# Retention and a Mish feed-forward on one core: two phases through HBM, or one interleaved loop kept on chip

## The chip, the core and the metric

The kernel runs on one core of a Trainium2 chip. A core has a matrix engine (TensorE, PE in the rows; its weight loads are shown as PEld), a vector engine (VectorE, DVE), an activation engine (ScalarE, ACT), a general engine (GpSimd, POOL) and a queue engine that only issues transfers (SyncE, SP). They run independently and wait for each other through semaphores. Matmuls write to PSUM, a small memory of eight banks; everything else lies in SBUF, and transfers (DMA) move data between SBUF and HBM. The metric is the device time of the whole program in microseconds (us), lower is better.

## What is computed

Eight batches of eight heads, 576 positions, head size 64. First a retention (attention without softmax, with a decay per head), then a feed-forward layer over all 4608 tokens with the Mish activation, `h * tanh(log(1 + exp(h)))`:

```python
scores = (q @ k.transpose(0, 1, 3, 2)) / sqrt(64)          # per batch b, head h: 576 x 576
gamma  = 1.0 - 2.0 ** (-5.0 - arange(8))                   # one decay per head
Dmat   = where(i >= j, gamma ** (i - j), 0.0)              # i: query position, j: key position
attn   = (scores * Dmat) @ v                               # 576 x 64 per head
x      = attn.transpose(0, 2, 1, 3).reshape(4608, 512)     # tokens x (head, dim)
h      = x @ w_in                                          # 512 -> 2048
out    = (h * tanh(softplus(h))) @ w_out                   # 2048 -> 512, float32
```

Inputs and output are float32; the kernel multiplies in bfloat16.

## The kernel before

One function with two phases, one after the other.

*Retention phase* (lines 50 to 126). A loop over the 8 heads builds `Lcat`, the decays of all distances of that head (L57 to L61). Inside, a loop over the 8 batches handles one (batch, head) pair, 64 in all. The 576 positions are cut into blocks of 128, 128, 128, 128 and 64. For each block `q` and `k` are loaded by POOL with a cast to bfloat16 (L74, L75), transposed on PE into one PSUM tile `tpqk` (L77, L78; a single buffer), and copied out by DVE (`qTall` L79, `kT` L81); `v` is loaded by SP (L84) and scaled by ACT (`vb` L86). Then PE computes the scores of each key block against all later queries (`Tp`, L99), DVE multiplies them by the decays (`Tm`, L104), PE multiplies with `vb` into five output tiles (`opsum`, L115), DVE copies them (L123), and SP stores them as 128 x 64 pieces into `x_bridge`, a float32 tensor in HBM (L124).

*Feed-forward phase* (lines 128 to 197). The weights are loaded by POOL with a cast, 64 pieces of `w_in` (L139) and 16 of `w_out` (L145). Then nine tiles of 512 tokens follow one another. A tile reads `x_bridge` back (L154), transposes it on PE (L157) and copies it out (`xs`, L158). Sixteen times, once for each 128 columns of the hidden layer, PE computes `hp` with four matmuls (L166) and DVE casts it to `hb` (L169). Mish is put together from `Exp` (L174), `Ln` with a bias of 1 (L179) and `Tanh` (L184) on ACT, and a product on DVE (`gT`, L189):

```python
for g in range(G): nc.scalar.activation(et, hbs[g], AX.Exp)
for g in range(G): nc.scalar.activation(lt, ets[g], AX.Ln, bias=1.0)
for g in range(G): nc.scalar.activation(tt, lts[g], AX.Tanh)
```

Then PE multiplies `gT` with `w_out` into four PSUM tiles `ops`, 64 matmuls (L191), DVE copies them (L196) and SP stores them (L197).

What sets the order: every engine executes its own instructions in order. A scheduler of the framework fixes that order from the dependencies, so it is not that of the program text: in the trace `Exp` and `Ln` calls are mixed. ACT loads a table of functions (`ACT_TABLE_LOAD`) when the next function isn't in the one it holds. A tile's name with `bufs=1` is one buffer: its next writer waits for its last reader.

Of the kernel before, what the change touches and what calls it, by code (L numbers as in the profile page):

```python
# [10 lines left out]
F32 = mybir.dt.float32  # L11
BF16 = mybir.dt.bfloat16
AX = mybir.ActivationFunctionType


@with_exitstack
def kernel(
# [8 lines left out]
):  # L26
    nc = tc.nc
    B, H, S, D = q.shape
    assert (B, H, S, D) == (8, 8, 576, 64)
    P = 128  # L30
    nblk = 5
    blks = [128, 128, 128, 128, 64]
    offs = [0, 128, 256, 384, 512]
    scale = 1.0 / math.sqrt(D)

    d_model = H * D
    n_tok = B * S
# [8 lines left out]
    Ntot = 640  # L46
    Ns = [576, 448, 320, 192, 64]
    with tc.tile_pool(name="attn_L", bufs=1) as Lpool, \
         tc.tile_pool(name="attn_io", bufs=3) as io, \
         tc.tile_pool(name="attn_work", bufs=3) as work, \  # L50
         tc.tile_pool(name="attn_psum", bufs=1, space=bass.MemoryType.PSUM) as pp, \
         tc.tile_pool(name="attn_opsum", bufs=1, space=bass.MemoryType.PSUM) as opp:
        for h in range(H):
            gamma = 1.0 - 2.0 ** (-5.0 - h)
            lg = math.log(gamma)
            Lcat = Lpool.tile([P, Ntot], F32, name="Lcat")
            nc.gpsimd.iota(Lcat, pattern=[[1, Ntot]], base=0,  # L57
                           channel_multiplier=-1,
                           allow_small_or_imprecise_dtypes=True)
            nc.scalar.activation(Lcat, Lcat, AX.Exp, scale=lg)  # L60
            nc.gpsimd.affine_select(  # L61
                out=Lcat[:, 0:P], in_=Lcat[:, 0:P],
                compare_op=mybir.AluOpType.is_ge,
                fill=0.0, base=0,
                pattern=[[1, P]], channel_multiplier=-1)

            for b in range(B):
                qTall = work.tile([D, Ntot], BF16, name="qTall", bufs=1)
                kT = []
                vs = []  # L70
                for j in range(nblk):
                    bl = blks[j]
                    qk_in = io.tile([P, 2 * D], BF16)
                    nc.gpsimd.dma_start(out=qk_in[:bl, 0:D], in_=q[b, h, ds(offs[j], bl), :])  # L74
                    nc.gpsimd.dma_start(out=qk_in[:bl, D:2 * D], in_=k[b, h, ds(offs[j], bl), :])  # L75
                    tpqk = pp.tile([D, 2 * P], BF16, bufs=1)
                    nc.tensor.matmul(tpqk[:, 0:bl], lhsT=qk_in[:bl, 0:D], rhs=ident[:bl, :bl], is_transpose=True, start=True, stop=True)  # L77
                    nc.tensor.matmul(tpqk[:, ds(P, bl)], lhsT=qk_in[:bl, D:2 * D], rhs=ident[:bl, :bl], is_transpose=True, start=True, stop=True)  # L78
                    nc.vector.tensor_copy(qTall[:, ds(128 * j, bl)], tpqk[:, 0:bl])  # L79
                    kt = work.tile([D, P], BF16, name=f"kT{j}", bufs=1)  # L80
                    nc.vector.tensor_copy(kt[:, 0:bl], tpqk[:, ds(P, bl)])  # L81
                    kT.append(kt)
                    vt = io.tile([P, D], F32)
                    nc.sync.dma_start(out=vt[:bl, :], in_=v[b, h, ds(offs[j], bl), :])  # L84
                    vb = work.tile([P, D], BF16, name=f"vb{j}", bufs=1)
# [142 lines left out]
```

## Time and profile before

| | |
|---|---|
| median of 3 runs | 1088.09 us (1086.58 to 1090.03) |
| profiled execution, first to last instruction | 1085.1 us |
| PE matmul / weight load busy | 690.4 / 330.5 us |
| DVE / ACT / POOL busy | 524.4 / 545.1 / 409.5 us |
| mean granted TensorE clock | 0.898 of full speed |
| transfers | 189895 packets, 47.54 MB |

Median and span are 3.0 us apart, which is what lies around the span. The times of a row of the profile are those of one instruction or of a group; "mean ns" is the mean of one, and the time of a matmul runs from its start to its modelled end, so that matmuls of a stream overlap and their spacing is smaller than their duration. "Granted clock" is the share of full speed that the chip allowed TensorE.

### The profile page before, as it was taken

What the parts mean: (1) busy time and instruction counts of PE and PEld (TensorE: products, weight loads), DVE (VectorE), ACT (ScalarE), POOL (GpSimd) and SP (SyncE); (2) the same over time, 40 slices, a digit from 0 to 9 for tenths busy, and PEclk for the clock granted to TensorE, in tenths of its full rate; (3) what the DMA queues carried; (4) which work ended last, traced back from release to release, by engine and by line L of the source; (5) the groups of instructions that cost most, each with busy time, mean ns of one, the idle gap of its engine ahead of it and who ended that gap; (6) DMA issues with size and microseconds to landing.
All of it is one profiled execution on the core that took longest, in us unless ns stands there. A gap on an engine that the chain in (4) does not pass through costs nothing.

```text
span 1085.1 us, 12380 instructions
## 1 busy us (share of the span) xinstructions
PE 690.4 (64%) x3254; PEld 330.5 (30%) x3280; DVE 524.4 (48%) x1812; ACT 545.1 (50%) x927; POOL 409.5 (38%) x778
## 2 busy tenths in 40 slices
PE   5776777777767767777617574738562919380915
PEld 2343334334333333433303232313221404130402
DVE  3665666566656556665505252525251616160613
ACT  2111111111111111111009989999699799969794
POOL 6666666666666666676496000000000000000000
PEclk9999999999999999999998796968695969695867
DMA  3444444444444444454378020202020111110101
GB/s 42 58 55 54 55 54 55 55 57 54 57 53 53 55 52 56 54 68 57 47 63 119 3 58 1 59 0 59 3 56 0 46 13 40 19 44 0 40 0 39
DMA packets 189895, 47.54 MB, mean 44 GB/s; under 512 B 178560, under 2 KB 185216, under 8 KB 189824
## 3 DMA queue, kind: packets, MB, share of 16 engines
q0 software_dynamic: 100672, 18.40, 21.1%
q1 hardware_dynamic: 89152, 28.35, 10.5%
q8 instruction: 25, 0.41, 0.2%
q14 instruction: 46, 0.38, 0.1%
HBM read 46.14 MB, written 18.87 MB: 60 GB/s over the span
## 4 chain that ended last, share of the span: by engine, by line
PE 44%; ACT 27%; DVE 15%; issue 5%; DMA 4%; POOL 4%; SPq 0%; DVEq 0%; POOLq 0%; ACTq 0%
PE ops L191 11%; PE Tp L99 11%; PE opsum L115 9%; ACT L179 8%; ACT L174 7%; ACT lt L179 6%; PE tpqk L77 5%; ACT et L174 5%; DVE qTall L79 5%; DVE Tm L104 4%; PE tpqk L78 4%; PE hp L166 3%; POOL win L139 3%; DVE kT L81 2%; DVE ot L123 1%
## 5 line engine op out<-in xcount | busy, mean ns | idle before, releaser
L86 ACT ACTIVATE vb<-vt 128x64 bf16<-128x64 f32 (+1 forms) x320 | 81.8, 256 | 436.1 <-PE opsum L115 363.5
L191 PE MATMUL ops<-wout,gT 128*128 128x512 bf16 x564 | 147.5, 418 | 184.0 <-DVE gT L189 166.5
L74 POOL DMA_DIRECT2D qk_in<-in_q_dram x320 | 173.7, 543 | 170.4 <-PE tpqk L78 84.4
L104 DVE TENSOR_TENSOR Tm<-Tp,Lcat 128x512 bf16<-128x512 f32 (+5 forms) x384 | 166.4, 434 | 73.8 <-PE Tp L99 58.7
L189 DVE TENSOR_TENSOR gT<-hb,tt 128x512 bf16<-128x512 bf16 x144 | 61.1, 424 | 256.7 <-ACT tt L184 198.5
L115 PE MATMUL opsum<-vb,Tm 128*128 128x64 bf16 (+2 forms) x960 | 151.9, 246 | 39.1 <-DVE Tm L104 39.1
L75 POOL DMA_DIRECT2D qk_in<-in_k_dram x320 | 174.3, 545 | 5.4 <-issue 5.4
L166 PE MATMUL hp<-xs,win 128*128 128x512 bf16 x562 | 147.5, 404 | 25.3 <-DMA win<-in_moe_w_in_dram 22.1
L154 POOL DMA_DIRECT2D xt<-x_bridge x36 | 19.2, 534 | 379.6 <-PE tp L157 373.2
L99 PE MATMUL Tp<-qTall,kT 64*128 64x512 bf16 (+5 forms) x384 | 140.9, 397 | 27.6 <-DVE qTall L79 21.5
L191 PEld LDWEIGHTS <-gT 128*128 128x128 bf16 x576 | 60.1, 106 | 268.1 <-DVE gT L189 207.3
L77 PE MATMUL tpqk<-ident,qk_in 128*64 128x128 bf16 (+1 forms) x320 | 87.4, 273 | 80.8 <-DVE kT L81 67.1
L174 ACT ACTIVATE et<-hb 128x512 bf16<-128x512 bf16 x144 | 84.1, 622 | 81.0 <-DVE hb L169 80.3
L169 DVE CAST hb<-hp 128x512 bf16<-128x512 f32 x144 | 98.5, 690 | 51.5 <-PE hp L166 51.0
L79 DVE COPY qTall<-tpqk 64x128 bf16<-64x128 bf16 (+1 forms) x320 | 66.5, 208 | 108.3 <-PE tpqk L78 103.7
L115 PEld LDWEIGHTS <-Tm 128*128 128x128 bf16 (+2 forms) x960 | 85.8, 119 | 107.8 <-DVE Tm L104 47.6
L179 ACT ACT_TABLE_LOAD x83 | 106.5, 1283 | 1.5
L78 PE MATMUL tpqk<-ident,qk_in 128*64 128x128 bf16 (+1 forms) x320 | 95.2, 298 | 5.0 <-DMA qk_in<-in_k_dram 4.9
L166 PEld LDWEIGHTS <-win 128*128 128x128 bf16 x576 | 57.9, 101 | 106.8 <-issue 28.5
L174 ACT ACT_TABLE_LOAD x68 | 87.2, 1283 | 1.2
L179 ACT ACTIVATE lt<-et 128x512 bf16<-128x512 bf16 x144 | 83.9, 622 | 0.9
L123 DVE COPY ot<-opsum 128x64 f32<-128x64 f32 (+1 forms) x320 | 63.5, 214 | 33.4 <-PE opsum L115 21.0
(22 smaller groups left out, 434.6 us busy)
## 6 DMA issues: line engine op xcount, KB each, us to landing
out_dram<-ot SPq DMA_DIRECT2D x36, 256.0 KB, 2.1
vt<-in_v_dram SPq DMA_DIRECT2D x256, 32.0 KB, 1.8
x_bridge<-ot SPq DMA_DIRECT2D x256, 32.0 KB, 1.6
xt<-x_bridge POOLq DMA_DIRECT2D x36, 128.0 KB, 3.0
qk_in<-in_q_dram POOLq DMA_DIRECT2D x256, 16.0 KB, 2.0
qk_in<-in_k_dram POOLq DMA_DIRECT2D x256, 16.0 KB, 2.1
win<-in_moe_w_in_dram POOLq DMA_DIRECT2D x64, 32.0 KB, 2.5
wout<-in_moe_w_out_dram POOLq DMA_DIRECT2D x16, 128.0 KB, 5.2
```

Of the source, the lines that this page charges most:

```text
L74: nc.gpsimd.dma_start(out=qk_in[:bl, 0:D], in_=q[b, h, ds(offs[j], bl), :])
L75: nc.gpsimd.dma_start(out=qk_in[:bl, D:2 * D], in_=k[b, h, ds(offs[j], bl), :])
L77: nc.tensor.matmul(tpqk[:, 0:bl], lhsT=qk_in[:bl, 0:D], rhs=ident[:bl, :bl], is_transpose=True, start=True, stop=True)
L78: nc.tensor.matmul(tpqk[:, ds(P, bl)], lhsT=qk_in[:bl, D:2 * D], rhs=ident[:bl, :bl], is_transpose=True, start=True, stop=True)
L79: nc.vector.tensor_copy(qTall[:, ds(128 * j, bl)], tpqk[:, 0:bl])
L99: nc.tensor.matmul(Tp[ds(0, blj), ds(0, w)], lhsT=kT[j][:, 0:blj], rhs=qTall[:, ds(128 * j + c0, w)], start=True, stop=True)
L104: nc.vector.tensor_tensor(Tm[ds(0, blj), ds(c0, w)], Tp[ds(0, blj), ds(0, w)], Lcat[ds(0, blj), ds(c0, w)], op=mybir.AluOpType.mult)
L115: nc.tensor.matmul(opsums[qi][ds(0, blq), :], lhsT=Tms[j][ds(0, blj), ds(128 * (qi - j), blq)], rhs=vs[j][ds(0, blj), :], start=(j == 0), ...
L166: nc.tensor.matmul(hp, lhsT=w_in_t[c][fg + g], rhs=xT[c], start=(c == 0), stop=(c == nK1 - 1))
L174: nc.scalar.activation(et, hbs[g], AX.Exp)
L179: nc.scalar.activation(lt, ets[g], AX.Ln, bias=1.0)
L191: nc.tensor.matmul(ops[s], lhsT=gT[:, ds(s * P, P)], rhs=w_out_t[ff], start=(ff == 0), stop=(ff == nF - 1))
```

## The change

The two phases become one loop, and nothing is stored between them. In the order of the new text:

- *Chunks.* The work is cut into 36 chunks of 128 tokens with all 8 heads. Each batch has four full chunks; the remaining 64 positions of two neighbouring batches make one chunk together (`c == 4`). Four chunks are a tile of the feed-forward, nine tiles in all.
- *Loads.* A chunk is loaded as three float32 tiles of 128 x (8 heads x 64), one DMA each on SP (`load`; two each where `c == 4`). They run seven chunks ahead (`PF = 7`, `bufs=8`). The weights come in four DMAs each on POOL, with the cast.
- *Scaling* (`prep`). `gamma ** (i - j)` is split into `gamma ** i` on `q` (DVE, with the factor 1/8) and `gamma ** -j` on `v` (POOL); `k` is cast by POOL. What is left of `Dmat` is a mask of zeros and ones.
- *Step T.* Eight 128 x 128 transposes (two heads each, for `q` and `k`) go to one PSUM bank; ACT copies all 1024 columns.
- *Step S.* Eight score matmuls with a 64-row contraction, alternately on rows 0 to 63 and 64 to 127 of the array, transposed (keys on partitions); DVE multiplies all 1024 columns by the mask. For `c < 4`, four matmuls add `k^T v` of the chunk to a state in PSUM.
- *Step O.* The state of the chunks before, masked to its diagonal blocks in SBUF, is applied by four matmuls (eight half-width ones where `c == 4`); eight matmuls with a 64-column stationary operand, alternately to output partitions 0 to 63 and 64 to 127, add the chunk's own part. The result has the features on partitions, which is the layout the feed-forward reads: DVE copies it into `xT`.
- *Feed-forward.* `g1(t, f)`: four matmuls into `hp`, then one ACT instruction `Mish` from PSUM to `gT`. `g2(t, i)`: four of the 64 matmuls with `w_out`; every fourth call ends a 128-token output tile in the one bank `ops`, which DVE copies and SP stores.
- *Order.* `tc.manual_schedule()` switches the framework's reordering off, so each engine runs its instructions in the order of the text. Four chunks go through T, S and O first. Then for each tile `t` and each `i` of 16: step T (at `i` = 0, 4, 8, 12), S (one later) or O (three later) of a chunk of tile `t + 1`, then `g1(t, i)`, then `g2(t - 1, i)`.

```diff
--- before.py
+++ after.py
...
-    x_dram = nc.dram_tensor("x_bridge", (n_tok, d_model), F32, kind="Internal")
...
+    NCH = 4
+    chunks = []
+    for b2 in range(0, B, 2):
+        for b in (b2, b2 + 1):
+            for c in range(4):
+                chunks.append((b, c))
+        chunks.append((b2, 4))
+    nT = len(chunks) // NCH
+    io = ctx.enter_context(tc.tile_pool(name="io", bufs=8))
+    tok = ctx.enter_context(tc.tile_pool(name="tok", bufs=3))
+    tr = ctx.enter_context(tc.tile_pool(name="tr", bufs=3))
...
+    ps_tp = ctx.enter_context(tc.tile_pool(name="ps_tp", bufs=1, space=PS))
+    ps_sc = ctx.enter_context(tc.tile_pool(name="ps_sc", bufs=1, space=PS))
+    ps_ot = ctx.enter_context(tc.tile_pool(name="ps_ot", bufs=1, space=PS))
+    ps_st = ctx.enter_context(tc.tile_pool(name="ps_st", bufs=1, space=PS))
+    ps_h = ctx.enter_context(tc.tile_pool(name="ps_h", bufs=2, space=PS))
+    ps_o = ctx.enter_context(tc.tile_pool(name="ps_o", bufs=1, space=PS))
+    ctx.enter_context(tc.manual_schedule())
+    def load(n):
+        b, c = chunks[n]
+        tiles = []
+        for nm, src in (("q", q), ("k", k), ("v", v)):
+            t = io.tile([P, H, D], F32, name=f"{nm}raw")
+            if c < 4:
+                nc.sync.dma_start(
+                    out=t, in_=src[b, :, ds(P * c, P), :].rearrange("h p d -> p h d"))
+            else:
+                for e in range(2):
+                    nc.sync.dma_start(
+                        out=t[ds(64 * e, 64)],
+                        in_=src[b + e, :, ds(512, 64), :].rearrange("h p d -> p h d"))
+            tiles.append(t)
+        raw[n] = tiles
+    PF = 7
+    for n in range(PF):
+        load(n)
...
+    gq = consts.tile([P, 5, H], F32)
+    gv = consts.tile([P, 5, H], F32)
+    nc.scalar.activation(gq, ex, AX.Exp)
+    nc.scalar.activation(gv, ex, AX.Exp, scale=-1.0)
+    nc.vector.tensor_scalar(gq, gq, 1.0 / math.sqrt(D), None, op0=OP.mult)
...
+    def load_w_in(i):
+        nc.gpsimd.dma_start(out=w_in_t[:, :, ts(i, 512)], in_=w_in_r[:, :, ts(i, 512)])
+    def load_w_out(i):
+        nc.gpsimd.dma_start(out=w_out_t[:, ts(i, 4), :], in_=w_out_r[:, ts(i, 4), :])
...
+    def prep(n):
+        b, c = chunks[n]
+        qr, kr, vr = raw.pop(n)
+        qs = tok.tile([P, H, D], BF16, name="qs")
+        ks = tok.tile([P, H, D], BF16, name="ks")
+        vs = tok.tile([P, H, D], BF16, name="vs")
+        nc.gpsimd.tensor_copy(ks, kr)
+        nc.vector.tensor_tensor(qs, qr, gq[:, c, :].unsqueeze(2).to_broadcast([P, H, D]), op=OP.mult)
+        nc.gpsimd.tensor_tensor(vs, vr, gv[:, c, :].unsqueeze(2).to_broadcast([P, H, D]), op=OP.mult)
+        live[n] = (qs, ks, vs)
+    def step_t(n):
+        qs, ks, vs = live[n]
+        tp = ps_tp.tile([P, 2, NP, P], BF16, name="tp")
+        for i, src in enumerate((qs, ks)):
+            flat = src.rearrange("p h d -> p (h d)")
+            for p in range(NP):
+                nc.tensor.transpose(tp[:, i, p, :], flat[:, ts(p, P)], ident)
+        qk = tr.tile([P, 2, NP, P], BF16, name="qkT")
+        nc.scalar.copy(qk, tp)
+        live[n] = (qk, ks, vs)
+    def step_s(n):
+        b, c = chunks[n]
+        qk, ks, vs = live[n]
+        sc = ps_sc.tile([P, 2, NP, P], F32, name="sc")
+        for p in range(NP):
+            for e in range(2):
+                r = ds(64 * e, 64)
+                nc.tensor.matmul(sc[:, e, p, :], lhsT=qk[r, 1, p, :], rhs=qk[r, 0, p, :],
+                                 start=True, stop=True)
+        sm = tr.tile([P, 2, NP, P], BF16, name="sm")
+        m = mask if c < 4 else mask2
+        nc.vector.tensor_tensor(
+            sm.rearrange("p e n i -> p (e n) i"), sc.rearrange("p e n i -> p (e n) i"),
+            m.unsqueeze(1).to_broadcast([P, 2 * NP, P]), op=OP.mult)
+        if c < 4:
+            if c == 0:
+                st_ps[b] = ps_st.tile([P, NP, P], F32, name="st")
+            st = st_ps[b]
+            kf = ks.rearrange("p h d -> p (h d)")
+            vf = vs.rearrange("p h d -> p (h d)")
+            for p in range(NP):
+                nc.tensor.matmul(st[:, p, :], lhsT=kf[:, ts(p, P)], rhs=vf[:, ts(p, P)],
+                                 start=(c == 0 and p == 0), stop=True, skip_group_check=True)
+        live[n] = (qk, sm, vs)
+    def step_o(n):
+        b, c = chunks[n]
+        t, s = divmod(n, NCH)
+        qk, sm, vs = live.pop(n)
+        ot = ps_ot.tile([P, NP, P], F32, name="ot")
+        first = True
+        if c > 0:
+            for p in range(NP):
+                halves = [(0, P, st_sb[b])] if c < 4 else [(0, 64, st_sb[b]), (64, 64, st_sb[b + 1])]
+                for i0, iw, ssb in halves:
+                    nc.tensor.matmul(ot[:, p, ds(i0, iw)], lhsT=ssb[:, p, :], rhs=qk[:, 0, p, ds(i0, iw)],
+                                     start=first, stop=False, skip_group_check=True)
+                    first = False
+        for p in range(NP):
+            for e in range(2):
+                nc.tensor.matmul(ot[ds(64 * e, 64), p, :], lhsT=vs[:, 2 * p + e, :], rhs=sm[:, e, p, :],
+                                 start=(first and p == 0), stop=True, skip_group_check=True)
+        if c < 4:
+            ssb = tr.tile([P, NP, P], BF16, name="ssb", bufs=4)
+            nc.vector.tensor_tensor(ssb, st_ps[b], diag.unsqueeze(1).to_broadcast([P, NP, P]), op=OP.mult)
+            st_sb[b] = ssb
+        if s == 0:
+            xts[t] = xp.tile([P, KC, NCH * P], BF16, name="xT")
+        nc.vector.tensor_copy(xts[t][:, :, ts(s, P)], ot)
...
+    def g1(t, f):
+        if f == 0:
+            gts[t] = gp.tile([P, nF, NCH * P], BF16, name="gT")
+        hp = ps_h.tile([P, NCH * P], F32, name="hp")
+        for c in range(KC):
+            nc.tensor.matmul(hp, lhsT=w_in_t[:, c, ts(f, P)], rhs=xts[t][:, c, :],
+                             start=(c == 0), stop=(c == KC - 1))
+        nc.scalar.activation(gts[t][:, f, :], hp, AX.Mish)
+    def g2(t, i):
+        s, part = divmod(i, 4)
+        if part == 0:
+            outs[t] = ps_o.tile([P, d_model], F32, name="ops")
+        ops = outs[t]
+        for f in range(4 * part, 4 * part + 4):
+            nc.tensor.matmul(ops, lhsT=gts[t][:, f, ts(s, P)], rhs=w_out_t[:, f, :],
+                             start=(f == 0), stop=(f == nF - 1))
+        if part == 3:
+            ot = op.tile([P, d_model], F32, name="res")
+            nc.vector.tensor_copy(ot, ops)
+            b, c = chunks[NCH * t + s]
+            if c < 4:
+                nc.sync.dma_start(out=out[ds(b * S + P * c, P), :], in_=ot)
+            else:
+                for e in range(2):
+                    nc.sync.dma_start(out=out[ds((b + e) * S + 512, 64), :], in_=ot[ds(64 * e, 64), :])
+    def att(n, step):
+        if n >= n_chunks:
+            return
+        if step == "T":
+            step_t(n)
+            if n + 1 < n_chunks:
+                prep(n + 1)
+            if n + PF < n_chunks:
+                load(n + PF)
+        elif step == "S":
+            step_s(n)
+        else:
+            step_o(n)
+    prep(0)
+    for i in range(4):
+        load_w_in(i)
+    for n in range(NCH):
+        att(n, "T")
+        att(n, "S")
+        att(n, "O")
+    for i in range(4):
+        load_w_out(i)
+    for t in range(nT + 1):
+        for i in range(nF):
+            ch, w = divmod(i, 4)
+            n = NCH * (t + 1) + ch
+            if t < nT:
+                if w == 0:
+                    att(n, "T")
+                elif w == 1:
+                    att(n, "S")
+                elif w == 3:
+                    att(n, "O")
+                g1(t, i)
+            if t > 0:
+                g2(t - 1, i)
...
```

More of the change, by code (lines that the diff above doesn't have):

```diff
@@ L13 @@
 AX = mybir.ActivationFunctionType
+OP = mybir.AluOpType
 @with_exitstack
@@ new lines @@
+    gv = consts.tile([P, 5, H], F32)
+    nc.scalar.activation(gq, ex, AX.Exp)
+    nc.scalar.activation(gv, ex, AX.Exp, scale=-1.0)
+    nc.vector.tensor_scalar(gq, gq, 1.0 / math.sqrt(D), None, op0=OP.mult)
+    mask = consts.tile([P, P], F32)
+    mask2 = consts.tile([P, P], F32)
+    nc.gpsimd.memset(mask, 1.0)
+    nc.gpsimd.affine_select(out=mask, in_=mask, compare_op=OP.is_ge, fill=0.0,
+                            base=0, pattern=[[1, P]], channel_multiplier=-1)
+    nc.gpsimd.tensor_copy(mask2, mask)
@@ new lines, in load_w_out @@
+    def load_w_out(i):
+        nc.gpsimd.dma_start(out=w_out_t[:, ts(i, 4), :], in_=w_out_r[:, ts(i, 4), :])
+    st_ps = {}
+    st_sb = {}
+    live = {}
+    xts = {}
+    def prep(n):
[8 more added lines that the diff above has]
+        live[n] = (qs, ks, vs)
@@ new lines @@
+    n_chunks = len(chunks)
+    def att(n, step):
[18 more added lines that the diff above has]
+        att(n, "O")
```

181 lines of the change are left out of this document (28 added, 153 removed).

## The prediction

> **What bounds the kernel now.** I read the page first: busy times, slices, and the chain that ended last.
>
> ```profile
> PE 690.4 (64%) x3254; PEld 330.5 (30%) x3280; DVE 524.4 (48%) x1812; ACT 545.1 (50%) x927; POOL 409.5 (38%) x778
> PE   5776777777767767777617574738562919380915
> ...
> ACT  2111111111111111111009989999699799969794
> ...
> PEclk9999999999999999999998796968695969695867
> ...
> PE 44%; ACT 27%; DVE 15%; issue 5%; DMA 4%; POOL 4%; SPq 0%; DVEq 0%; POOLq 0%; ACTq 0%
> ```
>
> No engine is the bound of the whole. The first 20 slices are the retention, with PE at seven tenths and ACT almost idle; the last 18 are the feed-forward, with ACT at nine tenths, PE coming and going and its clock falling. Next, the busy times by stage: retention, weight loading, feed-forward (columns: stretch, its length, busy time and count of PE, PEld, DVE, ACT, POOL, granted clock, DMA share, GB/s); below them one dense stretch of the feed-forward.
>
> ```profile
> 3.00:540.00 537.00, 385.28 (x1995) 201.05 (x1996) 323.23 (x1354) 86.78 (x327) 348.28 (x659) 1.00 0.46 54
> 540.00:586.00 46.00, 20.91 (x76) 7.74 (x77) 12.95 (x28) 16.20 (x21) 42.39 (x81) 1.00 0.77 83
> 586.00:1085.00 499.00, 284.24 (x1184) 121.68 (x1208) 188.23 (x431) 440.56 (x578) 16.44 (x31) 0.78 0.12 29
> ...
> 846.00:868.00 22.00, 20.12 (x94) 8.99 (x95) 16.24 (x37) 15.91 (x20) 1.59 (x3) 1.00 0.19 56
> ```
>
> So 537 + 46 + 499 us. The feed-forward is bound by ACT (440.6 of 499). What the retention waits for stands in the waits:
>
> ```profile
> DVE gT L189 <- ACT tt L184: 198.5, 18, 28.8
> PE ops L191 <- DVE gT L189: 166.5, 8, 29.3
> DVE qTall L79 <- PE tpqk L78: 103.7, 194, 5.2
> ...
> PE tpqk L77 <- DVE kT L81: 67.1, 188, 0.4
> ```
>
> The last two are one ping-pong over the single `tpqk` buffer: PE waits for DVE's copy, DVE for PE's transpose. The first two are PE waiting, through `gT`, for ACT, in eight waits of up to 29 us.
>
> **The change part by part.**
>
> *Mish.* ACT's instructions in the feed-forward:
>
> ```profile
> L179 ACT ACT_TABLE_LOAD x83 | 106.5, 1283 | 1.5
> L174 ACT ACT_TABLE_LOAD x68 | 87.2, 1283 | 1.2
> L174 ACT ACTIVATE et<-hb 128x512 bf16<-128x512 bf16 x144 | 84.1, 622 | 81.0 <-DVE hb L169 80.3
> ...
> L86 ACT ACTIVATE vb<-vt 128x64 bf16<-128x64 f32 x256 | 65.5, 256 | 387.8 <-PE opsum L115 363.5 <-DMA vt<-in_v_dram 19.3 <-issue 4.7
> ...
> L60 ACT ACTIVATE Lcat<-Lcat 128x640 f32<-128x640 f32 x8 | 5.9, 734 | 4.1 <-POOL Lcat L57 4.1
> L86 ACT ACT_TABLE_LOAD x1 | 1.3, 1283 | 0.8 <-PEq L212 0.8
> ```
>
> One `Mish` replaces three functions, some 150 table loads, and DVE's cast and product. I price it as `Exp`: 144 x 0.622 = 89.6 us. Step T's copy of 1024 columns follows from 256 ns at 64 and 734 ns at 640 columns, 0.83 ns a column: 734 + 384 x 0.83 = 1.05 us, x36 = 38 us. ACT falls to about 130 us: no longer a bound.
>
> *Feed-forward matmuls.* Still 1152 of 512 columns; this is the longest term. A warm stream in the chain, and the small matmuls of the retention:
>
> ```profile
> 1011.28 9.89 PE ops L191 x45
> ```
> ```profile
> 305.06 0.26 PE L77 MATMUL tpqk<-ident,qk_in 128*64 128x128 bf16 x1 [0.44 <-DVE kT L81]
> 305.12 0.31 PE L78 MATMUL tpqk<-ident,qk_in 128*64 128x128 bf16 x1
> ...
> 308.70 0.34 PE L115 MATMUL opsum<-vb,Tm 128*128 128x64 bf16 x3 [1.31 <-DVE Tm L104]
> 308.97 0.26 PE L78 MATMUL tpqk<-ident,qk_in 64*64 64x64 bf16 x1
> ```
> ```profile
> L115 PE MATMUL opsum<-vb,Tm 128*128 128x64 bf16 x640 | 91.0, 238 | 39.1 <-DVE Tm L104 39.1
> ```
>
> 9.89 / 45 = 0.220 us from one to the next (0.214 in the stretch 846 to 868), so 1152 x 0.220 = 253.4 us.
>
> *Retention matmuls.* 32 a chunk, all of 128 columns. Two such (305.06 and 305.12) stand 60 ns apart. Three of one array shape take 0.34 us; with 0.238 for the last that spaces them 50 ns, so the third starts at 308.80; the next, of another shape, starts at 308.97, 170 ns later. Hence 16 full-array matmuls (8 transposes, 4 state updates, 4 state applications) x 60 ns = 0.96 us; 16 half-array ones (8 scores, 8 outputs) at the same 60 ns = 0.96 us; four changes of shape (into and out of S, into and out of O's last eight) x 110 ns more = 0.44 us. Sum 2.36 us a chunk, for 32 chunks inside the loop 75.5 us. No row shows half-array matmuls that alternate between halves of the array: between 30 ns (both halves at work at once) and 170 ns (each a change of shape); I take 60, the row of the same shape.
>
> *Does anything stall PE in the loop?* Per chunk it has 32 x 0.220 + 2.36 = 9.4 us. The other engines, per chunk:
>
> ```profile
> L104 DVE TENSOR_TENSOR Tm<-Tp,Lcat 128x512 bf16<-128x512 f32 x64 | 44.2, 691 | 24.7 <-PE Tp L99 23.9 <-PE tpqk L77 0.8
> L104 DVE TENSOR_TENSOR Tm<-Tp,Lcat 128x64 bf16<-128x64 f32 x64 | 14.4, 225 | 12.7 <-PE Tp L99 12.6
> ...
> L196 DVE COPY ot<-ops 128x512 f32<-128x512 f32 x36 | 23.1, 684 | 4.6 <-PE ops L191 3.6 <-DMA out_dram<-ot 1.0
> ...
> L57 POOL IOTA Lcat<- 128x640 f32 x8 | 5.5, 693 | 0.0
> L61 POOL TENSOR_SCALAR_AFFINE_SELECT Lcat<-Lcat 128x128 f32<-128x128 f32 x8 | 2.4, 302 | 3.8 <-ACT Lcat L60 3.8
> ```
>
> DVE: four passes of 512 columns (`qs`, `ssb`, `xT`, `res`) at 0.69 and one of 1024 (the mask: 691 + 512 x 1.04 ns = 1.22 us): 4.0 us. ACT: 4 x 0.622 + 1.05 = 3.5 us. POOL: no row of a copy or a product; from 302 ns at 128 to 693 at 640 columns a pass of 512 is 0.6 us, and twice that with two inputs: 1.8 us. All below half of 9.4, so what counts is cover. S waits for T's copy: 0.1 + 1.05 + 0.1 us against eight 512-column matmuls (1.76 us), hidden; in tile 0 only four run between (0.88 us), so about 0.5 us is lost four times, 2 us. O waits for the mask product: 1.5 us against over 3 us. The single `ops` bank waits for a 0.69 us copy behind g1's 0.88 us and step T: hidden, but not after the last tile, where only g2 is left: 3 x 0.9 = 2.7 us. The next tile's first matmul needs the last `xT` copy, 0.9 us after O against 1.76 us.
>
> *Transfers.* The queues, and the issues with their time to landing:
>
> ```profile
> q0 software_dynamic: 100672, 18.40, 21.1%
> q1 hardware_dynamic: 89152, 28.35, 10.5%
> ...
> out_dram<-ot SPq DMA_DIRECT2D x36, 256.0 KB, 2.1
> vt<-in_v_dram SPq DMA_DIRECT2D x256, 32.0 KB, 1.8
> ```
> ```profile
> L197 SPq DMA_DIRECT2D out_dram<-ot x36: 332/332/462, 625.8 to 1081.7; - x36
> ```
>
> `x_bridge` (written, read and cast) goes. A chunk's loads are 3 x 1024 runs of 256 bytes. SP's queue took 10.5% x 16 x 1085.1 / 89152 = 20.4 ns a packet, and `vt` and `x_bridge` are such runs: 3072 x 20.4 / 16 = 3.9 us, hidden in 9.4. A store waiting on SP for `res` holds back the loads behind it, but those are seven chunks (66 us) ahead. The issue of one DMA of 1024 runs has no row: from 0.33 us (fixed, 128 runs) to 8 x 0.33 = 2.7 us (if by the run); three of the latter are 8.0 us, still under 9.4. I take the fixed cost, the nearest row; the other would delay the fourth chunk by some 9 us, once.
>
> *Start.* Nothing covers the first four chunks. Chunk 0 lands at about 1 + 1.8 + 3.9 = 7 us, scaling 2 us. T, copy, S, mask and O in a row are 0.6 + 1.25 + 0.6 + 1.4 + 1.1 = 5 us a chunk, 20 in all: 29 us at the earliest. `w_in` shares the transfer engines, so chunks 1 to 3 may take 7.8 us each, and the last ends at 7 + 23 + 7 = 37. I take 33. The weights, all of them, kept the engines at most 0.77 x 46 = 35 us (stretch 540 to 586); with eleven chunks of loads (43 us) that makes 78 us of work by the time `w_out` is first needed, at 33 + 14.1 + 9.4 + 2 = 58. Served last it would be 20 us late, served alternately not at all: 6 us.
>
> *Sum:* start 33 + matmuls 253.4 + chunks 75.5 + tile 0 2 + `w_out` 6 + end 2.7 and the last copy and store 0.9 + 2.1 + 3.0 outside the span (1088.09 less 1085.1) = 378.6 us.
>
> **The rivals.**
>
> *A, the halves overlap:* two half-array matmuls run at once, 30 ns each: 32 x 16 x 0.03 = 15 us less, 363. No row here has two halves in turn. [...]
>
> *B, the halves exclude each other:* each switch costs what a change of shape costs, 170 ns. 16 x 0.11 = 1.8 us more a chunk, 36 chunks: +63, 442. For it: the row at 308.97. Against: that is a change of size, not of place.
>
> *C, the table is swapped:* if `Mish` and the copy don't share a table, two loads of 1.28 us a chunk. ACT still fits (6.1 of 9.4), but the copy comes 1.28 us later than S's cover of 0.5 allows: 36 x 0.8 = 28 to, with both loads in the way, 75 us; I take 35, time 414. Against: one load at L86 served 320 copies beside eight `Exp`.
>
> *D, the clock:* in the feed-forward before, the granted clock was 0.78. PE's 329 us (253.4 + 75.5) at 0.78 are 422: +93, 472. Against: in the dense stretch 846 to 868 it was 1.00, and PE now has no wait of microseconds. [...]
>
> *E, slower than before:* the rearranged loads are not spread over the 16 engines. 36 x 3072 x 20.4 ns = 2256 us of transfer; on two engines 1128 us, over 1088, on three 752. Against: 128 runs of `vt` landed in 1.8 us, less than the 2.6 us that one engine would need for them, and the loads are still 128 partitions.
>
> **How the numbers follow.** My forecast 0.62, A 0.10, B 0.13, C 0.07, D 0.05, E 0.03. The prediction is the sum of the likeliest, 379. Low: A, with the start at 29 and `w_out` in time: 353. High: B, 442, which takes in C and the dearer issue of loads; outside remain D and E. All but E are faster by far more than the 0.3% that a measurement here can tell: 0.97; between two and three engines lies the small chance of no change.
>
> **What would show it.** Right: PE busy over 0.9 in the middle, granted clock near 1.00, 512-column matmuls 0.214 to 0.220 apart, about 39 us from one tile to the next (4 x 9.4 + small waits); two or three table loads; `x_bridge` gone; PE's longest waits at the start only. A and B show in the length of S and of O's last eight matmuls (0.25 us or 1.4 us for eight instead of 0.5); C in the count of table loads; the issue of loads in the duration of SP's DMA instructions; late weights as a PE wait for `w_out` about 58 us after the start. It is wrong if a tile takes over 46 us, or if the first feed-forward matmul starts after 45 us.

## The result and the profile after

The changed kernel took 357.77 us (median of four runs, 354.97 to 358.08) beside 1087.74 us for the kernel before (1086.58 to 1090.03): a ratio of 0.328 [0.327, 0.329]. The forecast was 379.0 us. The profiled execution took 358.08 us, its span is 356.4 us. In all runs below, only two count as slow (two of the six with the weights a quarter at a time), and their times are left out of the median there. First its page, the same parts as of before: busy times, slices, the chain that ended last, the costliest groups, the DMA issues (KB each, us to landing).

```profile
PE 318.4 (89%) x2231; PEld 161.8 (45%) x2272; DVE 137.3 (39%) x188; ACT 122.0 (34%) x184; POOL 67.9 (19%) x92
...
PE   2525948999999999999999999999999999999984
...
ACT  2111633433333333333334333333334333333200
...
PEclk9999987999999999999999999999999999999999
DMA  8999999999855555554555555654000001001012
...
PE 80%; SPq 9%; DMA 5%; ACT 2%; issue 1%; DVE 1%; POOL 0%; ACTq 0%; POOLq 0%
...
L230 ACT ACTIVATE gT<-hp 128x512 bf16<-128x512 f32 x144 | 86.2, 598 | 161.1 <-PE hp L228 154.5
...
L166 ACT COPY qkT<-tp 128x1024 bf16<-128x1024 bf16 x36 | 36.4, 1012 | 49.7 <-PE tp L164 49.7
...
vraw<-in_v_dram SPq DMA_DIRECT2D x32, 256.0 KB, 5.0
```

Before, no engine was the bound of the whole. Now PE is, from the seventh slice on: 80% of the chain, against 44%. ACT fell from 545.1 to 122.0 us. What is not PE in the chain (SP's queue 9%, DMA 5%) lies in the first slices, where the transfer engines are full. The same split by stage, with the columns of the stages of before (length, busy time and count of PE, PEld, DVE, ACT, POOL, granted clock, DMA share, GB/s): up to the first feed-forward matmul, tile 0, and one tile in the middle.

```profile
0.00:35.10 35.10, 13.71 (x132) 9.87 (x133) 14.88 (x30) 5.69 (x7) 15.00 (x28) 1.00 1.04 195
35.10:65.60 30.50, 23.95 (x188) 12.39 (x190) 13.16 (x18) 14.08 (x21) 9.96 (x13) 0.89 1.11 197
...
135.57:169.88 34.31, 33.95 (x249) 17.22 (x253) 15.02 (x19) 13.21 (x22) 6.60 (x8) 1.00 0.55 123
```

A middle tile is 33.95 of 34.31 us PE at full clock. The two stretches ahead of it are not: PE works 13.7 of 35.1 us and 24.0 of 30.5, with the transfers saturated (share 1.04 and 1.11). What PE waited for, in the whole run (total, times, longest):

```profile
PE st L190 <- POOL vs L155: 9.5, 2, 4.8
PE sc L176 <- ACT qkT L166: 5.4, 7, 1.2
PE tp L164 <- DVE qs L154: 4.9, 1, 4.9
PE ot L209 <- DVE sm L180: 4.7, 4, 2.7
PE ops L238 <- DVE res L242: 3.1, 4, 0.8
```

Before, PE's longest line was 166.5 us in eight waits of up to 29.3. Now a line is a handful of short ones. All but `ops` belong to the first 62 us; the four of `ops` are the end.

A chunk in the middle, from PE's timeline (start, length from first start to last end, count):

```profile
203.23 1.03 PE L228 MATMUL hp<-xT,w_in_t 128*128 128x512 bf16 x4
204.10 1.03 PE L238 MATMUL ops<-w_out_t,gT 128*128 128x512 bf16 x4
205.06 0.40 PE L176 MATMUL sc<-qkT 64*128 64x128 bf16 x8
...
209.07 0.39 PE L204 MATMUL ot<-qkT,ssb 128*128 128x128 bf16 x4
209.39 0.41 PE L209 MATMUL ot<-sm,vs 128*64 128x128 bf16 x8
```

Eight half-array matmuls (205.06, 209.39) take as long as four full-array ones: 0.40 us. In the records of single matmuls, the two halves of a pair start 4 ns apart and the next pair 53 ns later, 28 ns on average, where full-array ones are 56 ns apart. A change of array shape shows as a longer step: 0.96 us from 204.10 to 205.06 with four matmuls of 512 columns, where 203.23 to 204.10 is 0.87, so about 0.10 more.

### The profile page after: what moved, and what is told of

The parts are those of the page before. It is cut to its first block, busy times and chain, and to the rows that moved or that the text cites. A ratio compares the mean times of both kernels' runs of the same rounds, so it can differ in the third digit from the quotient of the medians.

```text
span 356.4 us, 5489 instructions
## 1 busy us (share of the span) xinstructions
PE 318.4 (89%) x2231; PEld 161.8 (45%) x2272; DVE 137.3 (39%) x188; ACT 122.0 (34%) x184; POOL 67.9 (19%) x92
## 3 DMA queue, kind: packets, MB, share of 16 engines
q1 hardware_dynamic: 117760, 37.76, 47.6%
## 4 chain that ended last, share of the span: by engine, by line
PE 80%; SPq 9%; DMA 5%; ACT 2%; issue 1%; DVE 1%; POOL 0%; ACTq 0%; POOLq 0%
PE ops L238 34%; PE hp L228 33%; SPq L84 9%; DMA vraw<-in_v_dram 5%; PE tp L164 4%; PE ot L209 3%; PE sc L176 3%; PE st L190 2%; PE ot L204 2%; ACT qkT L166 1%; DVE res L242 1%; ACT gT L230 1%; POOL vs L155 0%; ACTq L166 0%; POOLq L155 0%
## 5 line engine op out<-in xcount | busy, mean ns | idle before, releaser
L228 PE MATMUL hp<-xT,w_in_t 128*128 128x512 bf16 x551 | 147.4, 385 | 1.5 <-issue 0.4
L238 PE MATMUL ops<-w_out_t,gT 128*128 128x512 bf16 x560 | 142.9, 379 | 3.5 <-DVE res L242 3.1
L230 ACT ACTIVATE gT<-hp 128x512 bf16<-128x512 f32 x144 | 86.2, 598 | 161.1 <-PE hp L228 154.5
L228 PEld LDWEIGHTS <-w_in_t 128*128 128x128 bf16 x576 | 51.5, 99 | 49.9 <-issue 2.2
L180 DVE TENSOR_TENSOR sm<-sc,mask 128x1024 bf16<-128x1024 f32 x36 | 44.1, 1224 | 43.6 <-PE sc L176 41.3
L155 POOL TENSOR_TENSOR vs<-vraw,gv 128x512 bf16<-128x512 f32 x36 | 38.0, 1057 | 103.3 <-PE ot L209 67.1
L217 DVE CAST xT<-ot 128x512 bf16<-128x512 f32 x36 | 24.9, 692 | 76.3 <-PE ot L209 75.8
L166 ACT COPY qkT<-tp 128x1024 bf16<-128x1024 bf16 x36 | 36.4, 1012 | 49.7 <-PE tp L164 49.7
L242 DVE COPY res<-ops 128x512 f32<-128x512 f32 x36 | 24.9, 692 | 71.8 <-PE ops L238 69.5
L154 DVE TENSOR_TENSOR qs<-qraw,gq 128x512 bf16<-128x512 f32 x36 | 25.9, 720 | 21.4 <-DMA qraw<-in_q_dram 21.4
L176 PEld LDWEIGHTS <-qkT 64*128 64x128 bf16 x288 | 8.7, 99 | 20.6 <-ACT gT L230 11.9
L190 PEld LDWEIGHTS <-ks 128*128 128x128 bf16 x128 | 8.1, 104 | 13.2 <-issue 10.4
```

Source lines behind the costliest of these rows:

```text
L155: nc.gpsimd.tensor_tensor(vs, vr, gv[:, c, :].unsqueeze(2).to_broadcast([P, H, D]), op=OP.mult)
L166: nc.scalar.copy(qk, tp)
L176: nc.tensor.matmul(sc[:, e, p, :], lhsT=qk[r, 1, p, :], rhs=qk[r, 0, p, :], start=True, stop=True)
L180: nc.vector.tensor_tensor(sm.rearrange("p e n i -> p (e n) i"), sc.rearrange("p e n i -> p (e n) i"), m.unsqueeze(1).to_broadcast([P, 2 * ...
L190: nc.tensor.matmul(st[:, p, :], lhsT=kf[:, ts(p, P)], rhs=vf[:, ts(p, P)], start=(c == 0 and p == 0), stop=True, skip_group_check=True)
L228: nc.tensor.matmul(hp, lhsT=w_in_t[:, c, ts(f, P)], rhs=xts[t][:, c, :], start=(c == 0), stop=(c == KC - 1))
```

## The experiments

### Does the order of the halves matter?

```diff
-        for p in range(NP):
-            for e in range(2):        # step S, and the same in step O
+        for e in range(2):
+            for p in range(NP):
```

> The changed kernel with the score matmuls and O's last eight ordered by half: four on one half of the array, then four on the other, instead of in turn. Theory (rival A of the prediction: two halves work at once): the eight then stand about 56 ns apart instead of 4 and 53 in turn, so S and O cost 16 x 28 ns = 0.45 us more a chunk, 36 chunks 16 us: about 374 us against 357.8. If instead a half-array matmul is cheap in itself, whatever the order: 358.

Measured: 356.49 us, ratio 0.3277 [0.3269, 0.3285], the same as the changed kernel. PE's timeline of this run:

```profile
203.09 0.41 PE L176 MATMUL sc<-qkT 64*128 64x128 bf16 x8
```

Eight on one half after the other take the same 0.41 us, 28 ns from start to start on average, with single starts 13 and 43 ns apart in turn instead of 4 and 53. So these two orders cost the same. The run doesn't exclude that the halves overlap: the records don't say on which half a matmul worked, so how two halves would come to overlap in this order stays open. The next run asks directly whether they do.

### One half only

In S and O every second head is computed on the first half of the array instead of the second (in O not for `c == 0`).

```diff
-                r = ds(64 * e, 64)
+                r = ds(0, 64)
...
-                nc.tensor.matmul(ot[ds(64 * e, 64), p, :], ...
+                nc.tensor.matmul(ot[ds(64 * (e if c == 0 else 0), 64), p, :], ...
```

> The changed kernel with all score matmuls on rows 0 to 63 of the array, and O's last eight all to output partitions 0 to 63 (where c > 0): as many matmuls of the same size, but only one half of the array at work; the second head of each pair is left out. Theory (two halves work at once, in whatever order they are issued): with one half there is nothing to overlap with, the eight stand 56 instead of 28 ns apart on average: 8 x 28 x 36 ns + 8 x 28 x 28 ns = 14 us, about 370 against 356. If a half-array matmul is cheap in itself: 356.

Measured: 368.92 us, ratio 0.3385 [0.3372, 0.3398]; 12 to 13 us more than the changed kernel run again (355.98 us, ratio 0.3273, the control below). Its timeline, then a middle tile by stage:

```profile
202.42 0.62 PE L176 MATMUL sc<-qkT 64*128 64x128 bf16 x8
```
```profile
138.97:174.82 35.85, 35.49 (x249) 18.75 (x253) 15.02 (x19) 13.21 (x21) 6.61 (x8) 1.00 0.53 118
```

The same number of matmuls, but eight on one half take 0.62 us instead of 0.40, their starts 56 ns apart like those of full-array ones, and a tile 35.85 instead of 34.31 us. This shows the overlap: 1.54 us a tile, over 8 tiles 12.3 us, which is the difference.

### Two half shapes side by side

O of a chunk and S of the next one stand together, so that two of the four changes of shape become one between half shapes. T comes one chunk earlier.

```diff
+    att(NCH, "T")
+    att(NCH, "S")
...
                 if w == 0:
-                    att(n, "T")
-                elif w == 1:
-                    att(n, "S")
+                    att(n + 1, "T")
                 elif w == 3:
                     att(n, "O")
+                    att(n + 1, "S")
```

> S of the next chunk follows directly on O of this one, so that O's 64-column matmuls and S's 64-row matmuls stand side by side: three changes of array shape a chunk instead of four. Theory: a change costs some 95 ns (148 to 152 ns from the last of one shape to the first of another, against 56): 32 x 0.095 = 3 us less in the loop, and one more chunk's T and S (1.3 us) moves to the start: about 355 to 356 against 357. Rival: a change from one half shape straight to another costs as much as two: 357.

Measured: 354.82 us, ratio 0.3259 [0.3251, 0.3266], beside the control's 0.3273 [0.3267, 0.3279] on the same chip: the medians differ by 1.2 us, and the intervals lie only 0.0001 apart, so on the whole time the gain is barely clear.

```profile
207.70 0.41 PE L209 MATMUL ot<-sm,vs 128*64 128x128 bf16 x8
208.04 0.40 PE L176 MATMUL sc<-qkT 64*128 64x128 bf16 x8
```
```profile
135.38:169.27 33.89, 33.89 (x254) 17.56 (x253) 14.25 (x20) 13.22 (x22) 6.39 (x8) 1.00 0.55 125
```

A tile is 0.42 us shorter than in the changed kernel, 0.105 us a chunk. One change of shape fewer is worth 0.1 us: from O's last matmul to S's first it is 152 ns (0.34 us from first to first, 207.70 to 208.04), as much as from O to the next full-array matmul in the changed kernel (151 ns; 209.39 to 209.74). Part of the 3.4 us that eight tiles give is lost ahead of the loop, where T and S of one more chunk now stand (the first `Mish` starts at 40.1 us, against 37.8 in the changed kernel's profile and 36.3 in the control's).

### Mish alone, in the kernel before

```diff
-                    nc.vector.tensor_copy(hb, hp)
+                    nc.scalar.activation(hb, hp, AX.Mish)
...                                        # hb gets two buffers; Exp, Ln, Tanh and the product removed; gT = hbs[g]
```

> The kernel before with one part of the change alone: Mish as one ACT function from PSUM, in place of the cast, Exp, Ln, Tanh and the product. Theory: the feed-forward becomes bound by its matmuls, nine times 27.6 us plus about 2 us for transposes; retention 537 and weights 46 us stay: about 855 us. Rival: reading x_bridge back and the transposes stay in the open once ACT no longer covers them, 5 us a tile more: about 900.

Measured: 894.46 us, ratio 0.8228 [0.8209, 0.8247]: the rival's 900, not the theory's 855. The feed-forward stage of this run, then its waits:

```profile
586.00:893.00 307.00, 271.65 (x1205) 119.68 (x1202) 44.30 (x162) 76.43 (x128) 16.44 (x31) 0.92 0.20 47
```
```profile
PE tp L157 <- DVE xs L158: 22.3, 53, 1.4
...
PE hp L166 <- DMA win<-in_moe_w_in_dram: 21.5, 3, 7.3
```

ACT falls from 440.6 to 76.4 us in the stage, and the stage from 499 to 307. It is PE's now (271.7), with what the old order leaves open: PE waits for the copy of `xs` 53 times, and for weights. Mish alone is worth 193 us of the 730, the clock included, which rose from 0.78 to 0.92 in this stage.

### Three functions in the new order

`Mish` goes back to the cast on DVE, `Exp`, `Ln`, `Tanh` on ACT for four slices at a time, and the product on DVE.

```diff
-        nc.scalar.activation(gts[t][:, f, :], hp, AX.Mish)
+        nc.vector.tensor_copy(hb, hp)
+        pend.append((t, f, hb))
...                                        # flush() every four slices: four Exp, four Ln, four Tanh, then
+            nc.vector.tensor_tensor(gts[t][:, f, :], hb, tt, op=OP.mult)
```

> The changed kernel without native Mish: DVE casts, then Exp, Ln and Tanh, each for four hidden slices at a time, and a product on DVE. Theory: ACT becomes the bound: per chunk 12 x 0.61 + the copy 1.01 + two table loads 2.57 = 10.9 us against PE's 8.6, 36 x 10.9 = 392 + start 35 + end 20: about 445 us. If the copy and each of the functions swap the table, two more loads: 13.5 us a chunk, about 540. If ACT could still hide: 360.

Measured: 675.44 us, ratio 0.6213 [0.6199, 0.6228], 230 us above what was expected. The waits of PE and, in the second fence, of DVE:

```profile
PE hp L230 <- DVE hb L233: 247.1, 35, 9.0
```
```profile
DVE gT L253 <- ACT tt L250: 265.4, 36, 8.3
```

The products stand in DVE's order ahead of the next slice's cast, and wait for `Tanh`; PE waits for the cast, 7.1 us on average, 35 times. So this run measures an order of DVE's, not the price of three functions. With the product on POOL, that order is gone:

```diff
-            nc.vector.tensor_tensor(gts[t][:, f, :], hb, tt, op=OP.mult)
+            nc.gpsimd.tensor_tensor(gts[t][:, f, :], hb, tt, op=OP.mult)
```

> As the run with three functions, but the product on POOL, so that DVE's cast of the next hidden slice no longer stands behind a product that waits for Tanh. Theory: ACT alone is the bound, 12 x 0.617 + 1.01 + 2 x 1.28 = 11.0 us a chunk: 36 x 11.0 = 395 + start 35 + end 20: about 450 us, so native Mish is worth some 95 us in the new order. If the order of work around ACT, not its load, made the 675 us: over 600 again.

Measured: 455.87 us, ratio 0.4191 [0.4182, 0.4199]: 220 us back by moving one instruction; the clock's share is in it, 0.91 over the run instead of 0.80. The long middle by stage, then ACT's table loads:

```profile
60.00:340.00 280.00, 233.74 (x1556) 112.94 (x1585) 168.51 (x225) 250.56 (x378) 159.07 (x152) 0.92 0.45 98
```
```profile
L245 ACT ACT_TABLE_LOAD x36 | 46.2, 1283 | 0.6
L250 ACT ACT_TABLE_LOAD x36 | 46.2, 1283 | 0.6
```

ACT is the bound (250.6 of 280). In the new order, `Mish` is therefore worth 100 us (455.9 less 356.0), about half of its 193 in the old one.

### The phases apart

All 36 chunks first, then the feed-forward, everything still on chip (`xT` gets nine buffers).

```diff
-    for n in range(NCH):
+    for n in range(n_chunks):
...
-                if w == 0:
-                    att(n, "T")
...                                        # and no T, S, O in the loop over the tiles
```

> The changed kernel with the interleaving undone: all 36 chunks go through T, S and O first, then the nine tiles, nothing else changed. Theory: without matmuls to cover them the copies and the mask are waited for, 5.5 us a chunk (as chunk 1 of the changed kernel, 10.75 to 16.25 us after the start): 36 x 5.5 = 198, some 10 for the transfers of the start, then 250 + 9 x 1 + end 5: about 470 us. Rival: the waits are the start's transfers alone and a chunk needs its matmuls' 1.7 us and the 3.9 us of its loads: 140 + 26 + 262, about 430.

Measured: 455.36 us, ratio 0.4189 [0.4178, 0.42]. Its two stages, then PE's timeline in the first:

```profile
0.00:192.00 192.00, 109.99 (x1120) 81.87 (x1120) 118.75 (x151) 39.36 (x40) 69.82 (x92) 1.00 0.95 170
192.00:453.00 261.00, 253.32 (x1154) 112.76 (x1152) 25.61 (x37) 85.98 (x144) 0.00 (x0) 1.00 0.11 37
```
```profile
121.31 0.61 PE L164 MATMUL tp<-ident,qs 128*128 128x128 bf16 x4
121.71 0.63 PE L164 MATMUL tp<-ident,ks 128*128 128x128 bf16 x4
123.50 0.61 PE L176 MATMUL sc<-qkT 64*128 64x128 bf16 x8 [1.16 <-ACT qkT L166]
```

The retention alone, with nothing beside it, takes 192 us, nearer the theory's 198 + 10 than the rival's 166. Once the start is over the chunks stand 4.69 us apart. The transfer engines are nearly full in this stage (0.95), but the 4.69 us stay when the loads have ended (182.62 to 187.31, with a share of 0.26 from 150 to 190 us), so it is the chain of T, copy, S, mask and O that sets them. Interleaving is worth 99 us (455.4 less 356.0). Not only waits are covered by it: the four transposes take 0.61 us here and start 0.40 us after the four before, against 0.39 and 0.22 in the loop. That is nearly twice the spacing, although the clock column says 1.00. Moved between feed-forward matmuls, the same retention matmuls cost PE 1.70 us a chunk.

### The start: prefetch, order of the weights, bytes

The control is the changed kernel again, on the chip of the side-by-side shapes and of the next two runs (the one with fewer bytes ran on another).

> The changed kernel itself, for the others of this set to be compared with: 355 to 358 us by every theory.

Measured: 355.98 us (355.11 to 356.81), ratio 0.3273 [0.3267, 0.3279].

*Prefetch of three chunks:* `PF = 7` becomes `PF = 3`.

> Loads run three chunks ahead instead of seven. Theory: from the first feed-forward matmul (35 us) to the second tile (67 us) the transfer engines are full, and loads of chunks 8 to 13, not needed yet, take the place of w_out and of the chunks that are waited for; with three ahead the 4.8 us wait for v at 49 us shrinks and the half clock after it goes: about 350 us. In the loop three chunks (26 us) are ample for loads that land in 4 to 5 us: no new wait. Rival: the start is a chain of latencies and SP's issues, and less prefetch only makes loads later: 358 or more.

Measured: 356.06 us, ratio 0.3276 [0.3268, 0.3284]: no change. Its longest wait of PE in tile 0, then a load in the chain that ended last:

```profile
PE tp L164 <- POOL ks L153: 5.5, 4, 3.8
```
```profile
34.84 17.32 DMA vraw<-in_v_dram
```

The long wait moved from `v` to `k` of the same chunk, the seventh. Its `v` was issued at 34.84 us, at 34.86 in the changed kernel, and took as long to land. So the depth makes no difference here: SP's queue is behind in the start, and the loads of the first seven chunks are issued within 1 us of the control's. What loads that really run ahead would take from the near ones, this run doesn't show.

*Weights a quarter at a time:* each quarter of `w_in` is issued with one of the first four chunks, each quarter of `w_out` after one of tile 0's chunks, instead of four in a row.

```diff
-    for i in range(4):
-        load_w_in(i)
     for n in range(NCH):
+        load_w_in(n)
         att(n, "T")
...
-    for i in range(4):
-        load_w_out(i)
...
+                if t == 0 and w == 2:
+                    load_w_out(ch)
```

> Seven chunks ahead as before, but the weights one quarter at a time: w_in one quarter before each of the first four chunks, w_out one quarter per chunk of tile 0. Theory (transfers bind the start): w_out's burst no longer stops the loads that tile 0 waits for; the first feed-forward matmul starts at about 32 instead of 35 us, the second tile at about 62 instead of 66: about 353 us. Rival (the sum of bytes alone decides, 57 us of transfers before the second tile can start): 357, with the wait moved to w_out.

Measured: 347.53 us (median of four, 346.68 to 349.38), ratio 0.3198 [0.319, 0.3205], 8.5 us less than the control. The start and tile 0 of this run:

```profile
0.00:29.40 29.40, 13.65 (x132) 9.77 (x133) 14.67 (x29) 5.69 (x7) 12.28 (x25) 1.00 1.16 209
29.40:53.00 23.60, 22.61 (x192) 11.88 (x190) 13.02 (x17) 14.01 (x21) 10.23 (x13) 1.00 1.05 196
```

Beside the changed kernel's profile it is 5.7 us less before the first feed-forward matmul, 6.9 less in tile 0, and the clock there at 1.00 instead of 0.89. Some 4 us are given back in tile 1, where `w_out` is late: PE waits 2.1 us for it, and 3.4 us at half clock follow (four 512-column matmuls take 1.91 us at 63.84 and 1.03 at 67.78). So the long waits are loads behind a burst of weights.

*Fewer bytes:* `k` is not loaded; the cast reads `q`'s tile in its place.

> The changed kernel without the loads of k; k is taken from q's tile, so a third of the loaded bytes and of SP's issues is left out. Theory (transfers bind the start): each of the first chunks takes 2.6 instead of 3.9 us; until the second tile eight chunks and the weights are 8 x 2.6 + 25.6 = 46 instead of 57 us: first feed-forward matmul at about 29 instead of 35, the second tile's at about 56 instead of 64 us, total about 348. In the loop, no change: 34.4 us a tile. Rival (the chain T, copy, S, mask, O of about 5 us a chunk sets the start): 356.

Measured: 344.42 us (344.25 to 344.82), ratio 0.3167 [0.3162, 0.3171]. The first matmul of the feed-forward came at 29.3 us and tile 1 at 52.0; the middle tiles stay at 34.3 us. Leaving out a third of the loaded bytes is worth 11.6 us, all of it in the first two stretches: loading bounds the start, and nothing in the middle. A third of SP's issues went with the bytes, and the run doesn't tell the two apart.

### What beats both

The shapes side by side, the weights in quarters (`w_out` one step earlier, at `w == 0`), and the last tile's outputs in the two buffers of `hp`, which is free by then:

```diff
+            if t == nT - 1:
+                outs[t] = ps_h.tile([P, d_model], F32, name="hp")
+            else:
+                outs[t] = ps_o.tile([P, d_model], F32, name="ops")
```

> Weights one quarter at a time (w_out a little earlier than in the run with paced weights), S of the next chunk side by side with O, and the last tile's outputs in the two banks of hp instead of the one of ops, so that its matmuls need not wait for the copy. From the runs: 348.6 - 1.2 for the shapes - 3 x 0.8 at the end - 2 for the wait on w_out, if they add up: about 343 to 346 us. If the start gives back what the loop gains: 348.

Measured: 343.49 us (341.07 to 346.18), ratio 0.3158 [0.3141, 0.3176]. PE's timeline at the end, then its tile 0:

```profile
323.08 13.98 PE L241 MATMUL hp<-w_out_t,gT 128*128 128x512 bf16 x63
```
```profile
34.78:56.40 21.62, 21.46 (x181) 11.58 (x184) 12.21 (x16) 13.96 (x21) 8.57 (x11) 1.00 1.20 209
```

The last 64 matmuls run through in 13.98 us; tile 0 is 21.6 instead of 30.5 us long and PE is busy in all of it. The start gives some of this back: the first feed-forward matmul comes at 34.8 us, against 29.4 with the weights in quarters alone. PE now works 92% of the span.

## Why the prediction was right, and where it was off

The bound was forecast rightly, and one term of the sum was not. The time lies in the stated range because its low end was priced with rival A, to which the prediction gave a chance of 0.10; of the times it names, A's 363 is the nearest.

*The bound.* As forecast: one loop bound by PE, with the others below half of a chunk's time (ACT 13.2, DVE 15.0, POOL 6.6 us of 34.3 in a middle tile), and none of PE's listed waits in it. `Mish` at 598 ns was priced 622, step T's copy at 1012 ns 1050, the mask pass at 1224 ns 1220, POOL's two passes together 1.67 us 1.8. Only two tables were loaded, one at the start and one at `Mish`:

```profile
L112 ACT ACT_TABLE_LOAD x1 | 1.3, 1283 | 0.8 <-PEq L304 0.8
L230 ACT ACT_TABLE_LOAD x1 | 1.3, 1283 | 0.0
```

*Feed-forward matmuls.* Predicted 1152 x 0.220 = 253.4 us. In the loop they are 0.2157 us apart: 248.5, so 4.9 less. The row of before says the same: its 9.89 us hold the whole length of the last matmul (0.38), and 9.51 / 44 is 0.216.

*Retention matmuls: the term that was mis-sized.* Predicted 2.36 us a chunk, measured 1.70: a tile of 34.4 us (34.31 and 34.52 in turn) less 128 x 0.2157 = 27.6, by four. Its parts: full-array 16 x 56 ns = 0.90 (forecast 0.96), half-array 16 x 28 ns = 0.45 (0.96), four changes of about 95 ns = 0.38 (0.44). The step that failed is taking the row of the same shape, 60 ns, for matmuls that alternate between halves. Rival A's 30 ns, which no row of before shows, is what happened: 28 ns on average, and 56 in the run with one half alone. 32 x 0.66 = 21.1 us less. That 60 ns fit the full-array ones is luck: the two rows were half-array ones themselves (128*64), only the first step after a wait (58 ns in the changed kernel too, at 53.95, and 107 from there on), and, as the last section shows, at half clock.

*Start.* Predicted 33, measured 35.16. The size was near, with more against it than was forecast. PE's rows in the start and tile 0, then the chain's own row for the load of `v`, SP's timeline for an issue, and POOL's for the weights:

```profile
16.25 0.61 PE L164 MATMUL tp<-ident,qs 128*128 128x128 bf16 x4
...
25.29 0.59 PE L190 MATMUL st<-vs,ks 128*128 128x128 bf16 x4 [4.69 <-POOL vs L155]
...
29.61 0.61 PE L164 MATMUL tp<-ident,qs 128*128 128x128 bf16 x4
...
35.16 0.61 PE L228 MATMUL hp<-xT,w_in_t 128*128 128x512 bf16 x1
...
53.95 0.59 PE L190 MATMUL st<-vs,ks 128*128 128x128 bf16 x4 [4.76 <-POOL vs L155]
```
```profile
34.86 17.84 DMA vraw<-in_v_dram
```
```profile
14.05 6.46 SPq L84 DMA_DIRECT2D kraw<-in_k_dram  x1
```
```profile
33.79 3.04 POOL L139 DMA_DIRECT2D w_out_t<-in_moe_w_out_dram  x4
```

The fourth chunk's T (29.61) comes 13.4 us after the third's (16.25), where the others stand 5.5 to 5.9 apart. SP's issues of its `k` and `v` took 6.46 and 4.35 us; the prediction took 0.33 us an issue, and said that the dear issue would delay the fourth chunk by some 9 us, once. About that happened. So 33 came near as a value chosen between 29 and 37, not because its parts were right.

*Tile 0.* Predicted 2 + 6 = 8 us lost, measured 30.5 less 20.6 of PE work (64 x 0.2157 + 4 x 1.70) = 9.9. The 2, for S waiting on T's copy, were three times 0.3. And the 6 were for the wrong sub-step: PE never waited for `w_out`. It waited 4.76 us, at 54 us, for a load of `v` that was issued at 34.86, in the middle of `w_out`'s four issues (33.8 to 36.8), and landed 17.84 us later. The prediction had weights waiting behind loads; the loads waited behind the weights. The run with the weights in quarters shows that it is this order. Most of the rest is half clock: PE worked at it up to 37.8 us and from 54.0 to 58.2 (512-column matmuls 427 ns apart, 216 in between), 6.9 us in all, of which half is lost, 3.4. That 9.9 is near 8 is luck.

*End and outside.* Predicted 2.7 + 0.9 + 2.1, measured about 7.6 together. The bubbles were four of 0.78 us instead of three of 0.9: the first matmul after the last `g1` also finds `ops` still being copied. Here is the first of them in PE's timeline:

```profile
335.04 3.61 PE L238 MATMUL ops<-w_out_t,gT 128*128 128x512 bf16 x16 [0.78 <-DVE res L242]
```

Outside the span lay 1.7 us, not 3.0.

*The sum.* Start +2.2, matmuls -4.9, retention -21.1, tile 0 +1.9, end +1.9, outside -1.3: -21.3, so 378.6 becomes 357.3, beside 358.08 measured in that execution.

*The other rivals.* B (halves that exclude each other) would have made S 1.4 us long; it is 0.40. C (tables swapped) needed two loads a chunk; there was one for `Mish` in all. D (the clock) did not come in the loop, which stands at 1.00; it dips in tile 0, from within the 4.76 us wait on (0.50 from 51.5 to 58.2). With the weights in quarters tile 0 has neither, and the dip follows the 2.1 us wait of tile 1. The 1.00 in the row of the old retention (3 to 540 us) says nothing against D: as the last section shows, its matmuls ran at half clock. E (few transfer engines): a 256 KB load lands in 4 to 5 us at the median, and the share in a middle tile is 0.55.

*Where the 730 us came from.* Along one chain of runs: `Mish` alone 1087 to 894; chunks kept on chip, phases apart, 894 to 455; interleaving 455 to 356. Of the 439 in the middle, by stages: the retention 537 to 192 us, the stage that loads the weights 46 to nothing (they load under the retention), the feed-forward 307 to 261. That middle step changes many things at once (loads, scaling, chunks of all heads, no way through HBM); no run takes them apart.

## What to carry to other kernels

Here, matmuls that use half of the array cost half when both halves have work (28 ns against 56), in both orders tried; what is left to save beside them are the changes of shape, about 0.1 us each. When the loop is bound by one engine, look at the ends: here the order of two kinds of loads was worth 8 us, with no work changed. Before pricing a function by its engine time, see what stands behind its result on the next engine's queue: one product ahead of a cast cost 220 us.

## What the runs showed of the hardware beyond that

- *The clock column can miss a slow start.* Its first record in the changed kernel is at 37.76 us. Up to there it shows 1.00, although the matmuls stand as far apart as where it shows 0.50 (51.5 to 58.2 us): full-array ones of 128 columns 107 ns and those of 512 columns 427 ns, against 56 and 216 in the loop. The four transposes at 16.25 take 0.61 us, the length they have in the uncovered retention, not the 0.39 of the loop. The kernel before is such a case too: its first record is at 573 us, its 512-column matmuls are 427 ns apart just ahead of that and 215 right after, and the transposes of its retention last as long as those at half clock (0.31 us for one; 0.22 in the loop), although the column says 1.00 (308 ns on average in the row below). Take the clock from the length and spacing of matmuls where the column has not changed yet.
- *Issuing a transfer kept SP busy.* A load of 1024 runs of 256 bytes took SP at least 0.37 us, and up to 6.46 us while the transfer engines were full (issued at 14.05, with a share of 1.20 from 13 to 15 us). That is longer than the prediction's upper bound of 2.7.
- *A load landed very late.* Beside the weights' burst, a 256 KB load took 17.8 us, against a median of 5.0.

The transposes of `k` in the old retention, from the groups of the kernel before (count, busy time, mean ns):

```profile
L78 PE MATMUL tpqk<-ident,qk_in 128*64 128x128 bf16 x256 | 78.8, 308 | 4.2 <-DMA qk_in<-in_k_dram 4.1
```
